# Moving the reads of three range-check counts, reordering one chunk's products and sharing out PSUM copies, in a routed-attention and MLP-mixer kernel

## Chip, cores and metric

One NeuronCore of a Trainium2 chip. The metric is the device time of one execution in microseconds (us), the median of several runs. A profile is one more execution, recorded by the hardware profiler.

## The reference

Four batches, 8 heads, 768 positions, head size 64, in float32. The attention's output becomes the input of an MLP mixer. Setup and shapes are left out here.

```python
def _attn_ref(q, k, v, centroids):
    q_assign = np.argmax(np.einsum('bhsd,hcd->bhsc', q_n, c_n), axis=-1)   # 16 clusters
    k_assign = np.argmax(np.einsum('bhsd,hcd->bhsc', k_n, c_n), axis=-1)
    mask = q_assign[:, :, :, None] == k_assign[:, :, None, :]
    scores = np.where(mask, scale * np.matmul(q, k.transpose(0, 1, 3, 2)), -1000000000.0)
    attn = np.exp(scores - np.max(scores, axis=-1, keepdims=True))
    attn = attn / (np.sum(attn, axis=-1, keepdims=True) + 1e-09)
    return np.matmul(attn, v).astype(np.float32)

def _moe_ref(x, w_tok1, w_tok2, w_ch1, w_ch2):     # x: (4, 768, 512), the heads side by side
    xt = x.transpose(0, 2, 1)
    h = np.maximum(xt @ w_tok1, 0.0) @ w_tok2      # 768 -> 256 -> 768
    u = x + h.transpose(0, 2, 1)
    h2 = np.maximum(u @ w_ch1, 0.0) @ w_ch2        # 512 -> 1536 -> 512
    return (u + h2).astype(np.float32)
```

## The kernel before

The program is written out in order: every engine gets its instructions in the order of the source, and there is no loop at run time. It has four stages. Attention goes through 16 pairs of heads (scores, exponentials, values, sums). Then come the token products of all batches (`tok1`, `tok2`), which leave u in the SBUF tiles `xs[b]`, 128 partitions by 6 rows `j` by 512 channels. Then, for each batch b and each half `part` of the 1536 inner channels, three chunks of the first channel product (`ch1_chunk`, i = 0, 1, 2) and three of the second (`ch2_chunk`). Last comes a branch.

The two channel products use a Strassen-like scheme with seven half-size products in place of eight. `chunk` issues them in a set order through `product` and hands each finished PSUM tile to `done`. Its PSUM tiles have the tags X, Z and Y, each with two buffers. The products on X add up in one tile: A11·B11 (`p1`), then S2·T2 (`u2`), then S3·T3 (`c22`), then A22·T4 (`c21`). After each of the four, VectorE (in `ch2_chunk`) or ScalarE or VectorE (in `ch1_chunk`) reads the tile, and the next product on X can write only when that read is done. Between the products on X stand those on other tiles: S1·T1 (`p5`) and S4·B22 (`c12`) on Z, A12·B21 (`c11`) on Y. The last product of a chunk, A22·T4, isn't issued at the chunk's end: it is put in the list `late`, and the next chunk issues it behind its own first product. Only the very last chunk of the program has no successor. There line 886, `late.pop()()`, issues it directly behind S3·T3 on the same tile.

In `ch2_chunk`, each product is three matmuls in the program, six in the trace, with 256 columns. All of `done` is VectorE's (the helper lines 531 and 534 in the trace): `p1`, `p5` and `u2` are kept, `c11`, `c22`, `c12` and `c21` are added into rows of `xs[b]`. With part = 1, `c12` and `c21` each complete a row, and SP (the SyncE queue) sends it off with a DMA of 256 KB (line 703).

Before a batch's channel products, `turn_u(b, n)` transposes half n of u: for each of four channel blocks f, TensorE does three 128x128 transposes into a PSUM tile `pt` (tag Y, two buffers), and ScalarE copies the tile to `uT` (line 583). So block 2 has to wait until block 0 has been copied, and block 3 until block 1 has. With n = 1, four VectorE subtractions follow (lines 588 to 591). Batch 0 is turned among the token products. Batch b + 1 is turned inside the second channel product of batch b, behind its chunks 0 and 1 with part = 1, that is n = 0 and n = 1. It is done 8 times in all.

The range check decides whether the fast path's numbers can be trusted. `fits` counts on VectorE, `fits_count` adds up on TensorE and leaves three integers in `count`, both during batch 0. `fits_load` (line 733, with the reads on line 736) reads the three integers into a register of every engine. SP also checks their range there. It stands on line 887, behind everything else. On line 1070 every engine branches on their sum: with this data the branch skips `general()`, a slow path whose code lies between the branch and the program's end. At the end SP waits for its DMA queues, and all engines meet.

Of the kernel before, what the change touches and what calls it, by code (L numbers as in the profile page):

```python
# [16 lines left out]
B, H, S, D = 4, 8, 768, 64  # L17
# [3 lines left out]
DM = H * D  # L21
# [24 lines left out]
def kernel(  # L46
# [29 lines left out]
    nc = tc.nc  # L76
# [453 lines left out]
    def sub(dst, a, b):  # L530
        nc.vector.tensor_tensor(out=dst, in0=a, in1=b, op=ALU.subtract)

    def add(dst, a, b):
        nc.vector.tensor_tensor(out=dst, in0=a, in1=b, op=ALU.add)  # L534
# [36 lines left out]
    def turn_u(b, n):  # L571

        if n == 0:
            pools["uT"] = pools["u"].tile([P, 2, NF, HS], F32, name="uT")
            pools["uTs"] = pools["u"].tile([P, 3, NF // 2, HS], F32, name="uTs")
        uT, uTs = pools["uT"], pools["uTs"]
        for f in range(NF):
            pt = pools["ps_m"].tile([P, HJ, P], F32, tag="Y", name="pt")
            for i in range(HJ):
                nc.tensor.transpose(  # L580
                    out=pt[:, i], in_=xs[b][:, HJ * n + i, f * P : (f + 1) * P], identity=ident
                )
            nc.scalar.copy(out=uT[:, n, f], in_=pt.rearrange("p i t -> p (i t)"))
        if n == 1:
            R = {"B11": uT[:, 0, 0:2], "B21": uT[:, 0, 2:4], "B22": uT[:, 1, 2:4]}
            R["T1"], R["T2"], R["T4"] = (uTs[:, i] for i in range(3))
            R["T3"] = b12 = uT[:, 1, 0:2]
            sub(R["T1"], b12, R["B11"])
            sub(R["T2"], R["B22"], R["T1"])
            sub(R["T3"], R["B22"], b12)  # L590
            sub(R["T4"], R["B21"], R["T2"])
            pools["R"] = R

    late = []

    def chunk(n, product, done):


        def ptile(tag):
            return pools["ps_m"].tile([P, n], F32, tag=tag, name="p" + tag)  # L600

        X = ptile("X")
        product(X, "A11", "B11", True)
        if late:
            late.pop()()
        done("p1", X)
        Z = ptile("Z")
        product(Z, "S1", "T1", True)
        done("p5", Z)
        Y = ptile("Y")  # L610
        product(Y, "A12", "B21", True)
        done("c11", Y)
        product(X, "S2", "T2", False)
        done("u2", X)
        product(Z, "S4", "B22", False)
        done("c12", Z)
        product(X, "S3", "T3", False)
        done("c22", X)

        def end():  # L620
            product(X, "A22", "T4", False)
            done("c21", X)

        late.append(end)

    def ch1_chunk(part, i):
# [17 lines left out]
        def done(name, psum):  # L644
# [24 lines left out]
            else:  # L669
                a = h2["A12"][:, i]  # L670
                nc.scalar.activation(out=a, in_=psum, func=ACT.Relu)
                sub(h2["S4"][:, i], a, h2["S2"][:, i])

        chunk(HS, product, done)

    def ch2_chunk(b, part, i):

        h2, Bw = pools["h2"], pools["B"]
        u = {
            f"c{r + 1}{c + 1}": xs[b][:, HJ * r + i, 256 * c : 256 * c + 256]  # L680
            for r in range(2)
            for c in range(2)
        }
        kept = {}
        takes = {"p1": "c11", "p5": "c22", "u2": "c12"}
        gives = {"c11": "p1", "c22": "p5", "c12": "u2"}

        def product(psum, a, w, start):
            for k in range(3):
                nc.tensor.matmul(  # L690
                    psum, lhsT=h2[a][:, k, i * P : (i + 1) * P], rhs=Bw[w][:, 3 * part + k],
                    start=start and k == 0, stop=k == 2, skip_group_check=not start,
                )

        def done(name, psum):
            if name in takes:
                kept[name] = pools["mlp"].tile([P, DM // 2], F32, name=name, bufs=2)
                add(kept[name], psum, u[takes[name]])
            else:
                add(u[name], psum, kept[gives[name]] if name in gives else u[name])  # L700
                if part == 1 and name in ("c12", "c21"):
                    j = i + HJ * (name == "c21")
                    nc.sync.dma_start(
                        out[b].rearrange("(p j) m -> p j m", p=P)[:, j], xs[b][:, j]
                    )

        chunk(DM // 2, product, done)

    good = const.tile([P, 3], F32, name="good")
    count = const.tile([1, 3], I32, name="count")  # L710
# [22 lines left out]
    def fits_load():  # L733

        loaded = [
            nc.values_load(count[0:1, i : i + 1], min_val=0, max_val=P) for i in range(3)
        ]
        return loaded[0] + loaded[1] + loaded[2]
# [124 lines left out]
    while ends:  # L863
        for _ in range(-(-len(beside) // len(ends))):
            beside.pop(0)()
        ends.pop(0)()
        if len(ends) in (11, 9):
            turn_u(0, len(ends) == 9)
# [4 lines left out]
    for b in range(B):  # L873
        for part in range(2):
            for i in range(3):
                ch1_chunk(part, i)
                for _ in range(2):
                    if beside:
                        beside.pop(0)()
            for i in range(3):  # L880
                ch2_chunk(b, part, i)
                if part == 1 and i < 2 and b + 1 < B:
                    turn_u(b + 1, i)
            if b == 0:
                (fits_count if part else fits)()
    late.pop()()
    both = fits_load()


    def general():  # L890
# [209 lines left out]
```

## Time and profile before

| | |
|---|---|
| median of 7 runs | 877.89 us (877.67 to 877.96) |
| the profiled execution | 878.12 us |
| its span (first to last instruction) | 876.1 us |
| mean granted TensorE clock | 0.998 |
| attention and token stage, up to about | 421 us |
| channel products, to the last addition | about 421 to 868.8 us |
| behind the last addition, to the end of the span | 7.3 us |

"PE" is TensorE's matmuls, "PEld" its weight loads, "DVE" VectorE, "ACT" ScalarE, "SP" SyncE. A "q" behind an engine's name means its sequencer, where register loads, branches, semaphores and DMA issues stand. These aren't counted as busy time. A group's row gives the busy time or the mean of one, then the idle time of the engine ahead of it and what ended that. All starts are in us from the start of the span. The span leaves out 2.0 us of the profiled execution's own time.

### The profile page before, as it was taken

The numbers are of one execution on the slowest core, as the hardware profiler recorded it, in microseconds if no ns is written. First come the engines' busy times: TensorE is split into PE (matmuls) and PEld (weight loads), VectorE is DVE, ScalarE is ACT, GpSimd is POOL, SyncE is SP. The second block draws the span as 40 slices with busy tenths as digits, with TensorE's granted clock in tenths as the row PEclk, the third lists the DMA queues.
The fourth block names the chain that finished last, engine by engine and source line by source line (L and its number), as shares of the span: only waits on it lengthen the run. The fifth ranks groups of instructions, "written<-read, shape, count | busy, mean of one in ns | idle before, by whom it ended". The sixth has DMA issues, their size and how long they took to land.

```text
span 876.1 us, 11022 instructions
## 1 busy us (share of the span) xinstructions
PE 862.6 (98%) x4294; PEld 522.9 (60%) x4294; DVE 505.2 (58%) x848; ACT 298.3 (34%) x506; POOL 44.3 (5%) x40
## 2 busy tenths in 40 slices
PE   9999999999999999999999999999999999999996
PEld 4444444444444444444578686685876867768675
DVE  6798898788878862895453433423344333443332
ACT  4666566666555551321210211203112031130210
POOL 1010011000010000330000000000000000000000
PEclk9999999999999999999999999999999999999999
DMA  8655676554443130420000010000010000100001
GB/s 153 156 118 121 137 137 123 121 115 97 97 97 73 20 91 0 144 73 1 0 1 1 0 37 37 0 1 0 35 38 1 0 1 25 48 1 1 0 25 51
DMA packets 133275, 47.61 MB, mean 54 GB/s; under 512 B 122080, under 2 KB 126176, under 8 KB 133216
## 3 DMA queue, kind: packets, MB, share of 16 engines
q1 hardware_dynamic: 131616, 46.45, 23.3%
q8 instruction: 35, 0.57, 0.3%
q10 hardware_dynamic: 1600, 0.39, 0.2%
q14 instruction: 24, 0.20, 0.1%
HBM read 34.64 MB, written 6.29 MB: 47 GB/s over the span
## 4 chain that ended last, share of the span: by engine, by line
PE 94%; DVE 4%; ACT 1%; issue 0%; DMA 0%; DVEq 0%
PE sc L416 18%; PE av L439 15%; PE pX L690 14%; PE pX L639 14%; PE pZ L690 7%; PE pZ L639 7%; PE ph L508 4%; PE pY L690 4%; PE pY L639 4%; PE pu L517 3%; PE px L468 1%; PE small L455 1%; PE pt L580 1%; PE small L296 1%; DVE wh L209 1%; DVE wT L214 1%
## 5 line engine op out<-in xcount | busy, mean ns | idle before, releaser
L421 ACT ACTIVATE ex<-sc 128x768 f32<-128x768 f32 x192 | 152.7, 813 | 44.8 <-PE sc L416 42.5
L416 PE MATMUL sc<-qkT 64*128 64x384 f32 x768 | 155.1, 482 | 0.0
L429 DVE TENSOR_TENSOR sum<-sum,ex 128x768 f32<-128x768 f32 x128 | 125.3, 979 | 13.8 <-ACT ex L421 0.5
L439 PE MATMUL av<-ex,va 128*64 128x384 f32 x768 | 130.9, 490 | 0.0
L439 PEld LDWEIGHTS av<-ex,va 128*64 128x64 f32 x768 | 52.2, 137 | 74.7 <-issue 71.0
L416 PEld LDWEIGHTS sc<-qkT 64*128 64x128 f32 x768 | 68.2, 188 | 34.8 <-issue 34.6
L639 PE MATMUL pX<-uT,wc 128*128 128x384 f32 x192 | 67.4, 487 | 0.0
L416 PE MATMUL sc<-ohT 64*128 64x384 bf16 x384 | 63.0, 324 | 0.3 <-DVE ohT L389 0.2
L647 ACT COPY p<-pX 128x384 f32<-128x384 f32 x24 | 11.4, 475 | 148.1 <-PE pX L639 148.1
L639 PEld LDWEIGHTS pX<-uT,wc 128*128 128x128 f32 x192 | 36.2, 190 | 24.7 <-issue 1.0
L221 POOL TENSOR_TENSOR wc<-wT,wup 128x512 int32<-128x512 int32 x24 | 32.1, 1337 | 253.5 <-ACT avT L446 132.0
L429 DVE TENSOR_TENSOR sum<-ex 128x768 f32<-128x768 f32 x32 | 32.1, 1002 | 20.3 <-ACT ex L421 20.2
L446 ACT COPY avT<-av 128x384 f32<-128x384 f32 x32 | 15.4, 480 | 83.0 <-PE av L439 83.0
L508 PE MATMUL ph<-x,wt 128*128 128x512 f32 x96 | 42.0, 594 | 1.2 <-DVE x L520 0.8
L517 PE MATMUL pu<-h,wt 128*128 128x512 f32 x96 | 42.0, 592 | 0.0
L534 DVE TENSOR_TENSOR c<-pZ,u 128x384 f32<-128x384 f32 x24 | 13.4, 558 | 46.8 <-PE pZ L639 46.8
L416 PEld LDWEIGHTS <-ohT 64*128 64x128 bf16 x384 | 19.2, 94 | 35.4 <-issue 13.6
L534 DVE TENSOR_TENSOR x<-pX,x 128x256 f32<-128x256 f32 x24 | 10.2, 424 | 49.3 <-PE pX L690 49.3
L534 DVE TENSOR_TENSOR hA<-pY,p 128x384 f32<-128x384 f32 x24 | 13.4, 557 | 40.4 <-PE pY L639 40.4
L690 PE MATMUL pX<-w2s,hA 128*128 128x256 f32 x144 | 35.1, 380 | 0.5 <-DVE x L534 0.5
L690 PE MATMUL pX<-wc,hA 128*128 128x256 f32 x144 | 35.0, 379 | 0.0
L690 PE MATMUL pZ<-w2s,hS 128*128 128x256 f32 x144 | 35.0, 379 | 0.0
(129 smaller groups left out, 1197.4 us busy)
## 6 DMA issues: line engine op xcount, KB each, us to landing
raw<-in_moe_w_ch_dram SPq DMA_DIRECT2D x24, 512.0 KB, 4.4
qk<-in_k_dram SPq DMA_DIRECT2D x64, 96.0 KB, 4.2
va<-in_v_dram SPq DMA_DIRECT2D x16, 384.0 KB, 4.0
out_dram<-x SPq DMA_DIRECT2D x24, 256.0 KB, 2.0
qk<-in_q_dram SPq DMA_DIRECT2D x60, 96.0 KB, 3.6
raw<-in_moe_w_tok_dram SPq DMA_DIRECT2D x3, 512.0 KB, 4.9
raw<-in_moe_w_tok_dram SPq DMA_DIRECT2D x4, 384.0 KB, 4.0
qk<-in_q_dram ACTq DMA_DIRECT2D x4, 96.0 KB, 3.4
```

Source lines behind the costliest of these rows:

```text
L221: nc.gpsimd.tensor_tensor(out=dst.bitcast(I32), in0=T, in1=up, op=ALU.add)
L416: nc.tensor.matmul(sc[:, h, 0:HS], lhsT=src[rows, 1, j], rhs=src[rows, 0, js], start=start, stop=not start,)
L421: nc.scalar.activation(out=ex, in_=sc[:, :, 0:HS], func=ACT.Exp, scale=SM_SCALE)
L429: nc.vector.tensor_tensor(out=acc, in0=acc if j > 1 else st["ex", 0], in1=st["ex", j], op=ALU.add)
L439: nc.tensor.matmul(av[h * D : (h + 1) * D], lhsT=st["va"][:, h, j], rhs=ex[:, h], start=(j == 0), stop=(j == NJ - 1),)
L446: nc.scalar.copy(out=st["avT"][:, js].rearrange("p j t -> p (j t)"), in_=av)
L508: nc.tensor.matmul(pf, lhsT=W["tok1"][:, j, t * P : (t + 1) * P], rhs=xs[b][:, j], start=(j == 0), stop=(j == NJ - 1),)
L517: nc.tensor.matmul(pu, lhsT=W["tok2"][:, t, j], rhs=h1s[b][:, t], start=(t == 0), stop=(t == NT - 1))
L534: nc.vector.tensor_tensor(out=dst, in0=a, in1=b, op=ALU.add)
L639: nc.tensor.matmul(psum, lhsT=A[a][:, k, c * P : (c + 1) * P], rhs=R[r][:, k], start=start and k == 0, stop=k == 1, skip_group_check=not s ...
L647: nc.scalar.copy(out=kept[name], in_=psum)
L690: nc.tensor.matmul(psum, lhsT=h2[a][:, k, i * P : (i + 1) * P], rhs=Bw[w][:, 3 * part + k], start=start and k == 0, stop=k == 2, skip_grou ...
```

## The change

Three edits. `turn_u`'s copies of the odd blocks f = 1 and f = 3 go from ScalarE to VectorE. In the very last chunk only (batch 3, part 1, i = 2), the products come in the order p1, (c21 of the chunk before), p5, u2, c11, c22, c12, c21, where they came as p1, (c21 of the chunk before), p5, c11, u2, c12, c22, c21. So Y's product stands between u2 and c22, and Z's second one between c22 and c21. And `fits_load` is called ahead of the last chunk: on every engine the three reads stand behind its share of chunk 1 (the branch stays at the end). On SP they now stand between the third and the fourth of batch 3's six output DMAs, on TensorE and VectorE ahead of the last chunk's instructions.

```diff
-            nc.scalar.copy(out=uT[:, n, f], in_=pt.rearrange("p i t -> p (i t)"))
+            copy = nc.vector.tensor_copy if f % 2 else nc.scalar.copy
+            copy(out=uT[:, n, f], in_=pt.rearrange("p i t -> p (i t)"))
...
-    def chunk(n, product, done):
+    def chunk(n, product, done, last=False):
...
         Y = ptile("Y")
-        product(Y, "A12", "B21", True)
-        done("c11", Y)
+
+        def product_y():
+            product(Y, "A12", "B21", True)
+            done("c11", Y)
+
+        def product_z():
+            product(Z, "S4", "B22", False)
+            done("c12", Z)
+
+
+        between = [product_y, product_z]
+        if not last:
+            between.pop(0)()
         product(X, "S2", "T2", False)
         done("u2", X)
-        product(Z, "S4", "B22", False)
-        done("c12", Z)
+        between.pop(0)()
         product(X, "S3", "T3", False)
         done("c22", X)
+        if last:
+            between.pop(0)()
...
-        chunk(DM // 2, product, done)
+        chunk(DM // 2, product, done, b == B - 1 and part == 1 and i == 2)
...
             for i in range(3):
+                if b == B - 1 and part == 1 and i == 2:
+                    both = fits_load()
                 ch2_chunk(b, part, i)
...
     late.pop()()
-    both = fits_load()
```

## Prediction

> **What bounds the kernel now.** I first read the page's busy times and the chain that ended last:
>
> ```profile
> PE 862.6 (98%) x4294; PEld 522.9 (60%) x4294; DVE 505.2 (58%) x848; ACT 298.3 (34%) x506; POOL 44.3 (5%) x40
> PE 94%; DVE 4%; ACT 1%; issue 0%; DMA 0%; DVEq 0%
> ```
>
> TensorE sets the time nearly everywhere, so an edit that leaves its matmuls alone can gain only where TensorE stands still, or behind its end. I looked for both. First the timeline of the last 12 us, TensorE and VectorE (start, duration):
>
> ```profile
> 863.47 1.46 PE L690 MATMUL pZ<-wc,hS 128*128 128x256 f32 x6
> 864.77 1.46 PE L690 MATMUL pX<-wc,hS 128*128 128x256 f32 x6
> 866.74 1.56 PE L690 MATMUL pX<-w2s,hA 128*128 128x256 f32 x6 [0.52 <-DVE x L534]
> 866.26 0.42 DVE L534 TENSOR_TENSOR x<-pX,p 128x256 f32<-128x256 f32 x1 [0.87 <-PE pX L690]
> 868.34 0.42 DVE L534 TENSOR_TENSOR x<-pX,x 128x256 f32<-128x256 f32 x1 [1.65 <-PE pX L690]
> ```
>
> The last product waits for VectorE's reading of pX. Everything is computed at 868.76, yet the span is 876.1: 7.3 us follow. What fills them stands in the rows of the count reads (line 736) and of the branch (line 1070), by sequencer, with min/median/max in ns and the first and last start:
>
> ```profile
> L736 PEldq TENSOR_LOAD <-count x3: 299/306/497, 866.8 to 867.8; - x3
> L736 DVEq TENSOR_LOAD <-count x3: 306/383/558, 868.4 to 869.4; - x3
> L736 SPq TENSOR_LOAD <-count x3: 262/282/521, 869.2 to 870.7; - x3
> ...
> L1070 SPq EVENT_SEMAPHORE  x8: 17/17/17, 874.2 to 874.7; - x8
> L1070 ACTq COMPARE_BRANCH  x1: 50/50/50, 843.0 to 843.0; - x1
> L1070 ACTq EVENT_SEMAPHORE  x1: 17/17/17, 845.4 to 845.4; - x1
> L1070 PEldq COMPARE_BRANCH  x1: 3321/3321/3321, 868.3 to 868.3; - x1
> L1070 DVEq COMPARE_BRANCH  x1: 72/72/72, 869.9 to 869.9; - x1
> L1070 SPq FUSED_REGOPS  x1: 43/43/43, 871.2 to 871.2; - x1
> L1070 SPq COMPARE_BRANCH  x1: 58/58/58, 871.3 to 871.3; - x1
> L1070 PEldq EVENT_SEMAPHORE  x1: 51/51/51, 871.6 to 871.6; - x1
> L1070 DVEq EVENT_SEMAPHORE  x1: 21/21/21, 872.9 to 872.9; - x1
> ```
>
> SP is the last. It issues the last output DMA at 868.8 (332 ns), reads the counts from 869.2 until 871.2, branches at 871.3, does nothing until 874.2, then waits for its DMA queues and meets the others at 876.1. The other engines are through their branch by 872.9. The last transfer took 2.8 us to land, at 871.6, so it isn't what SP waits for.
>
> **The reads moved ahead.** On SP the stretch from 869.2 to 871.2 goes: -2.0 us. In their new place the reads stand behind the DMA of chunk 1's c12. Its addition ends at 856.3 and the DMA's issue at 856.7; with 2.0 us of reads SP is free at 858.7, and the next DMA needs it only when c21 of chunk 1 is added, at 860.2: covered by 1.5 us. The counts themselves were written in batch 0, so the reads wait for nothing. On VectorE they take 1.4 us (868.4 to 869.8) behind an addition issued at 857.20, and the next instruction, that c21, starts at 859.79: covered by 1.2 us. ScalarE and GpSimd have no work there. On TensorE they take 1.3 us (866.8 to 868.1) in front of chunk 2's first product, which is to start at 857.00, with its weights 0.2 earlier. They needn't interrupt: in the rows above the first one starts at 866.8, when the last product's six matmuls have only just been let go at 866.74, so six matmuls (1.3 us) were already handed over. In the new place the product ahead is let go when VectorE has read pX, at 855.03. If the queue takes it at once, the reads run from 855.1 to 856.4 and cost nothing. If it holds only six matmuls, they start at 855.70 and end at 857.0, so the weights come 0.2 late. So 0 to 0.2, below nothing excluded because TensorE has no idle time there to win; I take 0.1, since the row shows a queue at least as deep as the worse case and no limit. [...]
>
> **The last chunk reordered.** Products in an undisturbed row start 1.295 us apart (857.00 to 864.77 in six), so c21's would start at 864.77 + 1.295 = 866.06 and not at 866.74: 0.68. Behind a stall it is also slower: its addition starts 1.60 after it, the one before 1.49: 0.11. Together -0.8 us. Does the new order wait elsewhere? u2 would start at 860.88 and needs p1's reading of pX, which ended at 860.13 + 0.41 = 860.54; the weights are wanted at 860.67, so a release as quick as the last one (866.68 to 866.74) is just in time. c22 at 863.47 needs u2's addition (862.38 to 862.80), c21 at 866.06 that of c22 (864.97 to 865.39): both covered by 0.6. c12's DMA moves from 865.4 to 866.7 and has left SP by 867.1, ahead of the last, now at 868.0.
>
> **The branch afterwards.** SP branches behind the last DMA, at 868.5 in place of 871.3. The gap behind it was 2.9 us on SP (871.3 to 874.2), 2.4 on ScalarE with no transfer about, 3.0 on VectorE while the last output was on its way, 3.3 on TensorE. SP now branches with that output on its way, so I take VectorE's 3.0: +0.1, between -0.5 and +0.4. The output lands at about 868.0 + 2.8 = 870.8, SP goes on at 871.5: hidden by 0.7.
>
> **Copies by two engines.** Does this close the gap in `turn_u`? One turn on TensorE, ScalarE and VectorE, and the one VectorE copy of that shape (line 771):
>
> ```profile
> 746.60 0.82 PE L580 MATMUL pt<-ident,x 128*128 128x128 f32 x6
> 747.66 0.93 PE L580 MATMUL pt<-ident,x 128*128 128x128 f32 x6 [0.24 <-ACT uT L583]
> 747.13 0.86 ACT L583 COPY uT<-pt 128x384 f32<-128x384 f32 x2 [8.92 <-PE pt L580]
> 748.02 0.96 DVE L531 TENSOR_TENSOR uTs<-uT 128x768 f32<-128x768 f32 x1 [0.80 <-ACT uT L583]
> 752.08 0.41 DVE L534 TENSOR_TENSOR p<-pX,x 128x256 f32<-128x256 f32 x1
> L771 DVE COPY qkT<-pt 128x384 f32<-128x384 f32 x1 | 0.6, 558 | 0.3 <-PE pt L371 0.3
> ```
>
> The gap ends when ScalarE has copied block 0 (747.13 + 0.48), and block 0 stays ScalarE's: nothing is gained there. Block 3 waits for block 1. Now that copy ends at 747.13 + 0.86 = 747.99. By VectorE it starts when block 1 is transposed, 746.60 + 0.82 = 747.42, plus 0.04 as on ScalarE, and takes 0.56: 748.02. So block 3 is let go 0.03 later, in 8 turns +0.2. Bounds: with ScalarE's duration of 479 ns it would come 0.05 earlier, -0.4 in all; delayed behind another addition by 0.03 more, +0.5. [...]
>
> With n = 1, VectorE's copy of block 3 now stands ahead of the four subtractions. It ends at about 749.2 (transposes end at 748.59, plus 0.04 and 0.56), and the first subtraction starts there, not at 748.02; the second can't start before the first has ended, at 750.1, where it was 749.14. All behind it comes 1.0 later: p1 ends not at 752.49 but at 753.5, and u2's product on the same tile is to start at 753.61. That cover of 1.1 is used up. I take +0.1 for the three turns (0 to 0.4).
>
> **Sum.** -2.0 -0.8 +0.1 +0.1 +0.2 +0.1 = -2.3 us: a profiled execution of 878.12 - 2.3 = 875.8 with a span of 873.8. The median lies 0.2 under the profiled execution's time, so 877.89 - 2.3 = 875.6. Best ends: -2.8 -0.5 -0.4 = -3.7, 874.2. Worst: -2.8 +0.4 +0.2 +0.5 +0.4 = -1.3, 876.6. Both need every bound at once, so this case's own range is 874.5 to 876.5.
>
> **Rivals.** I call a difference of up to 0.2% (1.76 us) no change, about what a measurement of this kernel can tell.
> - *SP's gap grows* (15%). With nothing in front of it, SP's branch meets the last two outputs and TensorE's and VectorE's gaps. For it: the last DMA took 2.8 us to land, the one before it 2.0, when gaps began beside it. Against it: VectorE's own gap beside that output was 3.0. If SP gets on only some time after the output has landed (870.8 + 2 = 872.8 in place of 871.5), 1.3 of the gain is gone: 876.9, no change.
> - *The turns' gap closes* (4%). If two engines let TensorE run on without the 0.24 us gap and its slow restart (1.06 between the two groups of six, where the second group takes 0.77), 8 x 0.3 to 0.4 more are won: 872.8. Against it: block 0's copy is unchanged.
> - *VectorE's copies hold TensorE up* (3%, the slower side). In order behind additions, and beside ScalarE reading PSUM, block 1's copy comes late, and each 0.1 us costs 0.8 over 8 turns. It decides from 0.55 us a turn on ((2.5 + 1.76) / 8): 879.7 or more. Against it: VectorE is idle from 747.22 to 748.02, just there.
> - *It doesn't do what it says*: TensorE or VectorE might now branch last. TensorE's branch moves up to about 866.1 and VectorE's to 867.7, so they are through by 870.7, ahead of SP. I leave it without a chance of its own.
>
> **How the numbers follow.** The forecast has 78%; with the closed gap and a little of its own range lost beyond 876.13, faster by over 0.2% gets 0.78, no change 0.19, slower 0.03. The range 874.5 to 876.5 leaves out the rivals.
>
> **What would show it.** In the profile after: no idle time at the last product; SP's branch within 0.2 us of the last DMA's issue and its next instruction about 3.0 us later; TensorE going on at 857 in the last chunk without a gap; in each turn the 0.24 us gap still there, released by ScalarE, and the first subtraction behind a VectorE copy. A gap of SP's over 4 us, a TensorE idle time in front of the last chunk's first product, or idle time over 0.5 us in the turns would make the prediction wrong.

## The result and the profile after

| | before | changed |
|---|---|---|
| median | 877.89 us (877.52 to 878.63, 35 runs) | 875.62 us (875.25 to 876.46, 15 runs) |
| span of the profiled execution | 876.1 us | 873.7 us |
| ScalarE, VectorE busy | 298.3, 505.2 us | 291.8, 513.2 us |

The ratio is 0.9974, with a 95% interval from 0.9967 to 0.9981: faster by 2.3 us, between 1.7 and 2.9. The small end lies just below the 1.76 us that the prediction calls no change. The forecast was 875.6.

The end of the changed kernel, TensorE and VectorE in order of time (start, duration):

```profile
862.66 1.46 PE L703 MATMUL pY<-wc,hA 128*128 128x256 f32 x6
863.95 1.46 PE L703 MATMUL pX<-wc,hS 128*128 128x256 f32 x6
865.25 1.46 PE L703 MATMUL pZ<-wc,hS 128*128 128x256 f32 x6
866.54 1.46 PE L703 MATMUL pX<-w2s,hA 128*128 128x256 f32 x6
```

```profile
868.04 0.42 DVE L534 TENSOR_TENSOR x<-pX,x 128x256 f32<-128x256 f32 x1 [0.87 <-PE pX L703]
```

The last product now follows at the undisturbed 1.29 us, without idle time, and lasts 1.46 instead of 1.56. From its start to the last addition there are 1.50 us, as behind the other undisturbed products (1.49 to 1.50). The rows of the reads (now line 749) and of the branch (now line 1084), with min/median/max in ns and the first and last start:

```profile
L749 PEldq TENSOR_LOAD <-count x3: 306/307/496, 855.6 to 856.6; - x3
L749 SPq TENSOR_LOAD <-count x3: 266/288/510, 857.2 to 858.7; - x3
L749 DVEq TENSOR_LOAD <-count x3: 306/308/689, 857.7 to 858.8; - x3
```

```profile
L1084 SPq EVENT_SEMAPHORE  x8: 17/17/17, 871.7 to 872.3; - x8
...
L1084 PEldq COMPARE_BRANCH  x1: 3784/3784/3784, 866.0 to 866.0; - x1
...
L1084 DVEq COMPARE_BRANCH  x1: 72/72/72, 868.1 to 868.1; - x1
...
L1084 SPq COMPARE_BRANCH  x1: 58/58/58, 869.0 to 869.0; - x1
L1084 PEldq EVENT_SEMAPHORE  x1: 51/51/51, 869.9 to 869.9; - x1
L1084 DVEq EVENT_SEMAPHORE  x1: 21/21/21, 871.1 to 871.1; - x1
```

SP issues its last DMA at 868.5, branches at 869.0 and goes on at 871.7. It is still the last, and TensorE and VectorE are through before it. Between the last addition's end and the span's end lie 5.2 us, where it was 7.3.

A turn with n = 1 in the changed kernel, TensorE and then VectorE:

```profile
746.99 0.82 PE L580 MATMUL pt<-ident,x 128*128 128x128 f32 x6
748.05 0.96 PE L580 MATMUL pt<-ident,x 128*128 128x128 f32 x6 [0.24 <-ACT uT L584]
...
752.73 1.46 PE L703 MATMUL pY<-wc,hA 128*128 128x256 f32 x6
754.02 1.52 PE L703 MATMUL pX<-w2s,hS 128*128 128x256 f32 x6
755.38 1.46 PE L703 MATMUL pZ<-wc,hS 128*128 128x256 f32 x6
```

```profile
747.84 0.56 DVE L584 COPY uT<-pt 128x384 f32<-128x384 f32 x1 [0.23 <-PE pt L580]
749.04 0.56 DVE L584 COPY uT<-pt 128x384 f32<-128x384 f32 x1 [0.64 <-PE pt L580]
749.52 0.95 DVE L531 TENSOR_TENSOR uTs<-uT 128x768 f32<-128x768 f32 x1
...
753.52 0.41 DVE L534 TENSOR_TENSOR p<-pX,x 128x256 f32<-128x256 f32 x1
```

The idle time of 0.24 us is still there and still ends with ScalarE's copy. The second half now lasts 0.96, where it was 0.93. p1 is read until 753.93, so the weights of u2's product can be loaded only just before it starts at 754.02 (in the trace that load waits 0.20 us for p1's reading), and the next product follows 1.36 later instead of 1.29.

### The profile page after: what moved, and what is told of

It reads as the page before. It is cut to its first block, busy times and chain, and to the rows that moved or that the text cites. A ratio compares the mean times of both kernels' runs of the same rounds, so it can differ in the third digit from the quotient of the medians.

```text
span 873.7 us, 11027 instructions
## 1 busy us (share of the span) xinstructions
PE 862.8 (99%) x4294; PEld 522.7 (60%) x4294; DVE 513.2 (59%) x864; ACT 291.8 (33%) x490; POOL 44.2 (5%) x40
## 4 chain that ended last, share of the span: by engine, by line
PE 95%; DVE 4%; ACT 1%; issue 0%; DMA 0%; DVEq 0%
PE sc L416 18%; PE av L439 15%; PE pX L703 14%; PE pX L652 14%; PE pZ L703 7%; PE pZ L652 7%; PE ph L508 4%; PE pY L703 4%; PE pY L652 4%; PE pu L517 3%; PE px L468 1%; PE small L455 1%; PE pt L580 1%; PE small L296 1%; DVE wh L209 1%; DVE wT L214 1%
## 5 line engine op out<-in xcount | busy, mean ns | idle before, releaser
L703 PE MATMUL pX<-w2s,hS 128*128 128x256 f32 x144 | 35.2, 380 | 0.0
```

The lines of the kernel that those rows point to most:

```text
L703: nc.tensor.matmul(psum, lhsT=h2[a][:, k, i * P : (i + 1) * P], rhs=Bw[w][:, 3 * part + k], start=start and k == 0, stop=k == 2, skip_grou ...
```

## The experiments

### One part taken out, or one part alone

Four kernels. One is the changed kernel without the copies:

```diff
-            copy = nc.vector.tensor_copy if f % 2 else nc.scalar.copy
-            copy(out=uT[:, n, f], in_=pt.rearrange("p i t -> p (i t)"))
+            nc.scalar.copy(out=uT[:, n, f], in_=pt.rearrange("p i t -> p (i t)"))
```

> The changed kernel with all of u's copies back on ScalarE; reads ahead and the new order stay. My theory: the copies by VectorE cost 0.03 us in each of 8 turns (block 3 let go later) and about 0.07 in each of three chunks behind a turn (p1 read late), 0.4 in all as the trace after shows, so this kernel is 0.4 faster than the changed one: 875.2, span 873.2. In its trace the second half of a turn again takes 0.77 and not 0.79, and no product waits for p1. Rival, the two engines gain or cost nothing and the 0.4 by which TensorE runs late before the last chunk is chance: 875.6, span 873.7.

The second is the kernel before with the reads moved alone:

```diff
             for i in range(3):
+                if b == B - 1 and part == 1 and i == 2:
+                    both = fits_load()
                 ch2_chunk(b, part, i)
...
-    both = fits_load()
```

> The kernel before with the reads of the three counts ahead of the last chunk, nothing else. My theory: SP's 2.0 us behind its last DMA go, TensorE and VectorE lose nothing: 877.9 - 2.0 = 875.9, with the last product still starting about 0.68 late. Rival, TensorE's share of the reads (1.3 us) holds up the last chunk's first product by up to 0.2, and SP's gap behind the branch grows beside the output by up to 0.4: 876.1 to 876.5. Second rival, the two gains overlap, so that the reads alone are worth the whole 2.3: 875.6.

The third is the kernel before with `chunk`'s `last` and the new order alone (that part of the diff above):

> The kernel before with the last chunk's products in the new order, nothing else. My theory: the stall in front of the last product goes, the last addition and the last DMA come 0.8 earlier, and all of SP's reads, branch and end with them: 877.9 - 0.8 = 877.1. Rival, the end is not set by that addition but by the branches of TensorE and VectorE or by a landing, and the gain is lost there: 877.9.

The fourth is the kernel before with the copies alone (the first part of the diff above):

> The kernel before with every other copy of u's transposes on VectorE, nothing else. My theory: +0.4 (8 x 0.03 and 3 x 0.07): 878.3, the 0.24 us idle time in each turn unchanged. Rival, the copies by two engines shorten the turns: the idle time of 0.24 us goes and 877.9 falls by up to 3.

| | median, us | before, us | difference | ratio, 95% interval |
|---|---|---|---|---|
| changed, no copies | 875.26 | 877.93 | -2.67 | 0.9970 (0.9958 to 0.9982) |
| reads alone | 876.23 | 877.93 | -1.70 | 0.9979 (0.9970 to 0.9988) |
| order alone | 877.13 | 877.93 | -0.80 | 0.9991 (0.9982 to 1.0000) |
| copies alone | 878.47 | 877.93 | +0.54 | 1.0006 (0.9997 to 1.0015) |

Reads, order and copies alone add up to -1.70 - 0.80 + 0.54 = -1.96, which fits the -2.3 of all three together within the intervals; these are wide, about 0.8 us each way. The traces are sharper: the parts' own steps (-2.1 behind the last addition, -0.8 in the last chunk, +0.4 in the turns) add up to -2.5, where the changed kernel's span fell by 2.4. So the parts hardly touch one another. The copies' medians alone don't prove a loss, since that interval holds 1; the traces do. Matmul by matmul, TensorE's starts against the kernel before move by about 0.03 in each of the eight turns and by 0.07 in each of three chunks with copies alone, 0.43 from the first turn's gap to the last chunk. Without the copies none of these steps is there.

Three of the four met their forecasts of 875.2, 877.1 and 878.3 within 0.2. The reads alone missed the 875.9 by 0.3. In that kernel's profile the first transposes, which wait for the first loads, started at 6.56 where it was 6.21, and all that follows is 0.4 later up to the last chunk. No instruction there differs from the kernel before. At its end, from the last addition (869.17) to the end of the span (874.4), 5.2 us are left of 7.3, so the reads' own gain is 2.1. Whether the median's 0.3 has the same cause the runs don't show; the interval (-2.6 to -1.1) holds 2.0.

### Four tiles for a turn

Two kernels give each of a turn's four blocks a PSUM tile of its own, in two banks that only attention and the small sums had used. The first copies all on ScalarE, the second keeps VectorE for the odd blocks.

```diff
-            pt = pools["ps_m"].tile([P, HJ, P], F32, tag="Y", name="pt")
+            if f < 2:
+                pt = pools["ps_m"].tile([P, HJ, P], F32, tag="Y", name="pt")
+            elif f == 2:
+                pt = ps_av.tile([P, HS], F32, name="av").rearrange("p (i t) -> p i t", i=HJ)
+            else:
+                pt = ps_w.tile([P, HJ, P], F32, tag="w", name="ptw")
```

> The changed kernel with all copies on ScalarE and a PSUM tile of its own for each of a turn's four blocks (the two spare banks that attention used), so that no transpose waits for a copy. My theory: the wait of block 2 for block 0's copy is what a turn loses, on whichever engine the odd blocks are copied. Then TensorE does twelve transposes in 1.3 us instead of 1.85 (0.39 at the gap, 0.1 behind it): 8 x 0.5 = 3.9 less, and 0.4 less for the copies back on ScalarE: 875.6 - 4.3 = 871.3. Rival, ScalarE's four copies (1.8 us) then become the wait of what comes next, the first products on uT or the subtractions, and half of it is given back: 873.

> The same four PSUM tiles, with the odd blocks' copies on VectorE as in the changed kernel. My theory: with no transpose waiting for a copy, block 3's lateness goes as well; what stays is the first subtraction behind VectorE's second copy, and as the transposes end 0.5 earlier that copy does too, so p1 comes at most as late as in the changed kernel against the product that needs it, which also starts 0.5 earlier: 871.3 to 871.6. Rival, two engines copying side by side are now what lets the next work start earlier: below 871.0.

Measured: 871.41 us with all copies on ScalarE (877.94 before; 0.9926, 0.9912 to 0.9940) and 871.28 with two engines (0.9925, 0.9911 to 0.9939). The two can't be told apart, and both beat the changed kernel by 4.2 to 4.3. A turn with ScalarE alone, TensorE:

```profile
742.71 0.82 PE L585 MATMUL pt<-ident,x 128*128 128x128 f32 x6
743.37 0.49 PE L585 MATMUL av<-ident,x 128*128 128x128 f32 x3
743.70 0.49 PE L585 MATMUL ptw<-ident,x 128*128 128x128 f32 x3
744.02 1.46 PE L707 MATMUL pX<-wc,hA 128*128 128x256 f32 x6
```

The next product starts 1.31 after the first transpose, where the changed kernel takes 748.84 - 746.99 = 1.85. So a turn lost 0.5 by waiting for copies. Of this 0.4 lies ahead of block 2's first transpose, which comes 748.05 - 746.99 = 1.06 behind the turn's start in the changed kernel and 0.66 here: that is the wait for block 0's copy, and no sharing of the odd blocks' copies could win it. These kernels free block 3 as well; the waits of blocks 2 and 3 weren't tried apart. With two engines the weights of u2's product still come late behind a turn with n = 1 (1.36 to the next product, not 1.29), because the four subtractions still stand behind VectorE's copy.

### Which copy costs what

The changed kernel with only block 1's copy on VectorE (`f == 1` in place of `f % 2`), and with only block 3's (`f == 3`):

> The changed kernel with only block 1's copy on VectorE, block 3's back on ScalarE. My theory: what VectorE's copies cost has two parts. Block 1's copy lets block 3 go 0.03 later in each of 8 turns; block 3's copy, ahead of the subtractions, makes p1 late by 0.07 in three chunks. Here the first stays and the second goes: 875.6 - 0.2 = 875.4, and in the trace block 3's transposes are 0.03 late while the product u2 behind a turn with n = 1 has no idle time. Rival, both parts come from block 1's copy: u2 still waits.

> The changed kernel with only block 3's copy on VectorE, block 1's back on ScalarE. My theory: the counterpart, block 3's transposes are let go as in the kernel before, and u2 behind a turn with n = 1 still waits 0.07: 875.4, by the trace 0.2 under the changed kernel in the stretch of the turns. Rival as for the kernel with block 1 alone.

Measured: 875.54 and 875.57 us (877.93 before; 0.9973 and 0.9972, both about 0.9962 to 0.9982), 0.05 to 0.08 under the changed kernel's 875.62 where 0.2 was expected; medians don't resolve that. The traces do. Waits of weight loads from 421 us to the last chunk, with block 3 alone:

```profile
PEld pt L580 <- ACT uT L584: 2.9, 6, 0.5
...
PEld pX L703 <- DVE p L534: 0.6, 3, 0.2
```

The three waits for p1 are there. With block 1 alone the list has no such line, and the second half of each turn lasts 0.96 again; with block 3 alone it lasts 0.93. TensorE's starts against the kernel before move by 0.21 over the eight turns with block 1 alone and by 0.20 over the three chunks with block 3 alone. So both parts stand as forecast: block 1's copy makes block 3 late, block 3's copy makes p1 late.

### The reads one product from the end

The changed kernel with `both = fits_load()` in front of the last `late.pop()()`, so in front of c21's product of the last chunk:

> The changed kernel with the reads moved from in front of the last chunk to in front of its very last product. My theory: what matters is where SP is free. Here SP's 2.0 us of reads start when c12's DMA has left it, about 867.5, and end at 869.6, where the last DMA could go at 868.5: 1.1 later, so 876.7. VectorE's reads (1.4 us behind an addition issued at 866.75) hold the last addition back by 0.1 to 0.2, which SP hides; TensorE's share again costs nothing, its queue being ahead. Rival, the reads cost only their place behind the last DMA, and anywhere ahead of it they are free: 875.6.

Measured: 876.95 us (877.94 before; 0.9988, 0.9979 to 0.9997), 1.3 over the changed kernel: "free anywhere ahead of the last DMA" falls. SP's last DMA, the reads and TensorE's products:

```profile
L716 SPq DMA_DIRECT2D out_dram<-x x1: 345/345/345, 869.8 to 869.8; - x1
...
DMA to landing us min/median/max: 4.2/4.2/4.2
```

```profile
L749 PEldq TENSOR_LOAD <-count x3: 306/306/495, 863.5 to 864.5; - x3
L749 DVEq TENSOR_LOAD <-count x3: 314/377/549, 866.9 to 867.9; - x3
L749 SPq TENSOR_LOAD <-count x3: 267/280/510, 867.7 to 869.1; - x3
```

```profile
862.76 1.46 PE L703 MATMUL pY<-wc,hA 128*128 128x256 f32 x6
864.05 1.46 PE L703 MATMUL pX<-wc,hS 128*128 128x256 f32 x6
865.35 1.46 PE L703 MATMUL pZ<-wc,hS 128*128 128x256 f32 x6
866.64 1.46 PE L703 MATMUL pX<-w2s,hA 128*128 128x256 f32 x6
```

VectorE's reads hold the last addition back to 868.34 (0.2 late), and SP, busy with its own, issues the last DMA at 869.8, 1.0 behind that addition's end. SP's branch comes at 870.3, 1.3 behind the changed kernel's, as the medians say. The landing, at 874.0, is here behind SP's gap (it goes on at 873.0) and sets the end of this execution; it took 877.62, 0.7 more than the kernel's median, so such a late landing needn't be the rule. TensorE loses nothing: its reads start at 863.5, in the middle of Y's product, and two whole products behind it still run before the one that the reads stand in front of. So at least 12 matmuls and the rest of Y's had been handed over ahead of the reads, more than the six that the trace before showed.

### A short jump

The changed kernel with the slow path left out; a memset that isn't executed stands in its place:

```diff
     with tc.If(both < 3 * P):
-        general()
+        nc.vector.memset(const.tile([P, 1], F32, name="nothing"), 0.0)
```

> The changed kernel with the slow path behind the branch left out: in its place stands one memset of 128x1 on VectorE, which isn't executed either with this data. The fast path, the reads and the branch stay. My theory: the gap behind the branch (2.75 on SP, 2.9 on VectorE, 3.8 on TensorE, 2.5 on ScalarE, but 0.2 on GpSimd, which has the fewest instructions in the slow path) belongs to the jump over the long slow path, and with a short jump it falls to GpSimd's 0.2. SP then waits for the last landing, 2.5 behind its issue: 868.5 + 2.55 = 871.0, where it went on at 871.7, so the span falls by 0.5 to 0.7: 875.0. Rival, the gap is the price of any branch that is taken with work around it: 2.75 stays, 875.6.

Measured: 873.05 us (877.93 before; 0.9948, 0.9934 to 0.9961), 2.6 under the changed kernel where 0.6 was expected. The branch and the DMAs from 867 us on:

```profile
L1084 DVEq COMPARE_BRANCH  x1: 72/72/72, 867.9 to 867.9; - x1
L1084 DVEq EVENT_SEMAPHORE  x1: 21/21/21, 868.3 to 868.3; - x1
...
L1084 SPq COMPARE_BRANCH  x1: 58/58/58, 868.7 to 868.7; - x1
```

```profile
L716 SPq DMA_DIRECT2D out_dram<-x x2: 332/332/332, 867.0 to 868.2; - x2
...
DMA to landing us min/median/max: 2.0/2.0/2.0
```

SP goes on 0.2 after its branch and VectorE 0.4, in place of 2.75 and 2.9. So the gap belongs to the long jump, not to the branch. The size was wrong because I had taken the landing as given. It falls from 2.5 (2.8 before) to 2.0 when no such gaps lie beside it (why, no run here shows), and of SP's waits for its DMA queues, eight in place of sixteen, all but two pass before the landing; in the changed kernel all sixteen (1.1 us, 871.7 to 872.9) came behind the gap. Behind the last addition 3.0 us are left of 5.2. The remaining 0.2 to 0.4 belong to nothing that was edited: TensorE runs 0.2 earlier in this profile from its first us on.

Packets of DMA queues that the profile marks "instruction" start in these gaps, in ScalarE's most plainly. In the kernel before, ScalarE branches at 842.96, such a packet, of 8 KB, starts at 843.90 and ScalarE goes on at 845.43; in the changed kernel the three are 843.44, 844.38 and 845.91. In each of the eleven profiles with the long jump one 8 KB packet starts inside ScalarE's gap, 0.9 to 1.2 us behind its branch, and ScalarE goes on 1.5 to 1.7 us behind the packet's start; in the three profiles where that packet starts latest (1.20) the gap is longest (2.72). With the short jump there is no instruction packet in that stretch, and none in any profile falls into GpSimd's 0.2. SP's gap holds three or four such packets while TensorE and VectorE stand behind their branches too. That an engine waited for one of them, no row shows.

## Why the prediction was right

Its terms against the traces, before to changed:

| term | forecast | measured |
|---|---|---|
| SP's reads | -2.0 | -2.06: from the end of the last DMA's issue to the branch, 2.21 us became 0.15 |
| the last chunk's order | -0.8 | -0.78 (order alone: median -0.80) |
| SP's gap behind the branch | +0.1 | -0.08 (2.83 became 2.75) |
| reads in TensorE's queue | +0.1 | 0 (857.48 - 856.18 = 1.30, undisturbed) |
| block 3 let go later, 8 turns | +0.2 | +0.21 (8 x 0.03) |
| p1 late, three turns | +0.1 | +0.21 (3 x 0.07) |
| a later start in attention, where no instruction differs | none | +0.06 |
| sum | -2.3 | -2.44 (spans 876.11 and 873.66) |

- **The two gains** came at their size, each alone and together, because SP ends the program: whatever leaves its queue behind the last addition counts in full, as long as the last output has landed by then (871.0 in the changed kernel, against 871.7). Their covers held as well. SP was through its reads at 859.2 and had the next DMA to issue at 860.7; VectorE was through at 859.2 and had its next addition at 860.3.
- **The gap behind the branch** was mis-sized. I gave SP VectorE's 3.0 because SP too would now branch with an output on its way; it kept its own value. In all eleven profiles with the long jump SP's gap was between 2.7 and 3.0, the transfers beside it notwithstanding. The first rival, a growing gap, falls.
- **TensorE's queue.** The row of six matmuls handed over was a lower bound, and I split the range for want of a better one. In the changed kernel the first read starts at 855.6, directly behind the reading of pX that lets chunk 1's c22 go (855.5) and 0.6 us ahead of that product's first matmul, so the queue took more than six. The run with the reads late shows at least 12. So the term is nothing. How much more the queue takes, no run shows.
- **The copies.** The term of block 3 was exact: the sixteen VectorE copies took 557 to 558 ns, the 558 of the one row before. p1's cover of 1.1 was used up as forecast. p1 was read 6.94 us after the turn's start (6.9 forecast), and u2's product followed at 7.03. So its weights could no longer be loaded ahead of time, and that cost 0.07 a chunk, where I had taken 0.03.
- **The rivals.** The turns' gap didn't close, for the reason given: block 2 waits for block 0, and block 0 stayed ScalarE's. VectorE's copies do hold TensorE up, by about 0.05 a turn on average, far from the point at which the change would have become slower: (2.5 + 1.76) / 8 = 0.53, which the prediction gives as 0.55.

Where the gains come from and what the copies cost was right. Three sizes were off: the gap (-0.2, and an output on its way was the wrong reason to choose VectorE's), TensorE's queue (-0.1) and p1 (+0.1). The spans fell by 2.44 and the medians by 2.27, where 2.3 was forecast. That 875.62 meets 875.6 so closely is partly luck: the profiled executions of these kernels lie up to 0.7 us from their kernels' medians.

## What to carry to other kernels

Follow the program past its last computation: the engine that ends last pays for each instruction there in full (here SP, 2.06 us for the reads of three counts with their checks), so reads and checks whose data lie ready belong where that engine has room, and their new place must leave it free when its next DMA falls due. Before a copy is shared out between engines, ask which copy the waiting work waits for; here it was the first of four, the edit moved the second and the fourth, and two more buffers won 0.5 us a turn where the sharing lost 0.05. A copy put in an in-order queue also delays all that stands behind it, so the reader of a PSUM tile several instructions on is part of its price (here p1's: read until 6.94 us after the turn's start where it was 5.89, 0.07 us a chunk).

## What the hardware showed unexpectedly

A branch over the long slow path kept SP from going on for 2.7 to 3.0 us, VectorE for 2.9 to 3.2, ScalarE for 2.5 to 2.7 and TensorE for 3.4 to 4.3, in every profile with it, though the branch instruction itself takes 57 to 72 ns on SP and VectorE; over a memset SP's was 0.2. GpSimd, with the shortest share of the slow path, had 0.2 over the long jump too. In the other engines' gaps instruction packets were on their way (by their starts, one in ScalarE's, two in TensorE's, three in VectorE's, and in SP's three in the kernel before and four in the changed one); with the short jump there were none. The last output took 2.0 us to land with the short jump and 2.5 to 3.2 with the long one, when such gaps lay beside it; the earlier outputs of the kernel before took 2.0 too. The 4.2 of the kernel with the late reads stands alone, and what made it so long stays open.
